# Fused attention and two feed-forward blocks: from step 21 the exponentials are transposed by VectorE and a trip through DRAM, not by TensorE

## The chip, the core and the metric

The program runs on one core of one Trainium2 chip. Its metric is device time in microseconds (us); the kernel before took 723.5 us (median of three runs, 723.3 to 726.39). The engines are named as in the profile: PE is TensorE's matmul pipe and PEld its weight loads, DVE is VectorE, ACT is ScalarE, POOL is GpSimd, and SP is the engine whose queue issues nearly all DMAs. Each engine works through its own instructions in a fixed order, and so does the queue of SP: an instruction that waits holds up all behind it.

## The reference, cut to what matters

```python
# q_l, k_l, v_l: 4 batches x 8 heads x 512 x 64;  q_g, k_g, v_g: 32 global tokens each
out_g = softmax(q_g @ [k_g, k_l].T / 8) @ [v_g, v_l]
s_ll  = where(|i - j| <= 32, q_l @ k_l.T / 8, -1e9)
out_l = softmax([q_l @ k_g.T / 8, s_ll]) @ [v_g, v_l]
x = concat(out_g, out_l)                 # 4 x 576 x 512
x = x + relu(layernorm(x) * g_ln @ w_ch1) @ w_ch2          # 512 -> 2048 -> 512
h = relu(x @ w_in)                                         # 512 -> 1024
c = conv over 3 neighbouring tokens of h, by channel (conv_w)
out = (h * sigmoid(c)) @ w_out                             # 1024 -> 512, all float32
```

A local query sees only 32 neighbours on each side and the 32 global keys. A tile of 128 queries thus needs 192 keys (an inner tile: 32 + 128 + 32) or 160 keys (an edge tile, the first and the last of a batch), and 32 global ones.

## The kernel before

The work is three overlapping parts. First, attention. It goes in *steps*: a `Local` step is a tile of 128 queries and one pair of heads, 64 of them (n = 0 to 63: batch, tile, pair), and a `Global` step is the 32 global queries of a batch and one pair, 16 of them, put between the local ones from n = 24 on. Steps 0 to 15 run alone at the start; the others run beside the second part. Second, the first network, in eight *chunks* of two or three tiles; each chunk goes through 16 blocks of weights (an *item* each: 12 matmuls into `ph`, ReLU by ACT into `hh`, the remainder into `hl` by DVE, then matmuls into `yps` one item later). Third, the second network.

A local step has these stages. The keys and queries are split into a high and a low part (`split`). PE writes the scores of both heads into `ps` (`products`), DVE adds the mask and finds the row's extreme (`sm`, `nm`), ACT makes the exponentials in place (`exps`). The values' product needs them with the keys on the partitions, so PE transposes `sm` against the identity, in three pieces of 128 keys for an edge tile and in four of 112 for an inner one (`turn`), ACT copies the result from PSUM to `ptsb` (`turned`), and PE multiplies it with `rawv` into `po` (`values`). After the fourth pair DVE divides by the sums and writes the tile `x` (`back`).

`add_step` says in which order the stages of neighbouring steps are written. In its step i it writes the scores of i, the transposes and the values of i-1 and the division of i-2, in four parts a to d. `tick` writes some of these parts after each piece of the first network, at a pace that gets a chunk's tiles ready by the chunk's start. All attention instructions get a priority that is 300 places ahead; a scheduler orders each engine's queue from priority, data and free buffers.

Tiles for the third chunk on are already transposed as the change does it: `cross` transposes the normalized tile in blocks of 32 x 32 on DVE into `stage`, a DMA writes it to DRAM (`way`), and four DMAs, one for each 32 partitions, read it back into `xn` with the blocks in their new places. There are 12 such trips. ACT and DVE then copy `xn` into `xe` or `xo`, the operand of `ph`.

Lines of the kernel before that the prediction speaks of: 321, 322 (scores), 325 (mask and extreme), 334 (exponentials), 347 (transposes by PE), 352 (their copy), 362 to 364 and 368 (values), 207, 210, 213 (the trip of `cross`), 109 (copies, of `xn` too), 760 (`ph`), 769 (`hh`), 770 (`hl`), 784, 785, 789 (`yps`), 164 (last use of the buffers `fpx` in converting weights). A matmul of float32 data such as the values' is two instructions in the trace; a transpose is one.

## Time and profile before

| | |
|---|---|
| three runs | 723.3, 723.5, 726.39 us |
| span of the profiled execution | 721.6 us (its own time is not listed apart; the median of the runs is 1.9 us longer than this span) |
| busy: PE, PEld | 709.5 us (98%), 637.1 us (88%) |
| busy: DVE, ACT, POOL | 455.8 us (63%), 424.0 us (59%), 173.2 us (24%) |
| mean granted TensorE clock | 0.999 of 2.4 GHz |
| chain that ended last | PE 87%, DMA 5%, DVE 2%, ACT 2% |
| DMA | 82.16 MB, mean busy share of the 16 engines 36% |

The profile is of one execution. A group of instructions has its count, its mean duration and the idle time of its engine just before it. A busy PE is not PE at its peak, since matmuls overlap: what one costs on a full PE is the distance from its start to the next start, and that is read from the timeline. In a row of the timeline the idle time stands at the end, with what ended it.

### The profile page before, as it was taken

Reading aid. Unit: us, or ns where it says so; the run is one execution under the profiler, and the core shown is the slowest. Engines: PE = TensorE matmul, PEld = TensorE weight load, DVE = VectorE, ACT = ScalarE, POOL = GpSimd, SP = SyncE. Lnnn points to the kernel's source line nnn. Section 1 sums busy time; section 2 is a strip of 40 time slices with the busy share of each in tenths; the row PEclk is TensorE's granted clock in tenths of the full one; section 3 lists DMA queues with packets and bytes.
Section 4 is the critical chain, followed back from the end, with each engine's and each line's share of the span. In section 5 each row is a group of like instructions: output and inputs, shape, how many; then the busy total and the mean of one; then the engine's idle time right before and its main releaser. Section 6 shows DMA issues by size and latency. Waiting matters only on the chain.

```text
span 721.6 us, 12952 instructions
## 1 busy us (share of the span) xinstructions
PE 709.5 (98%) x4617; PEld 637.1 (88%) x4617; DVE 455.8 (63%) x1132; ACT 424.0 (59%) x1003; POOL 173.2 (24%) x236
## 2 busy tenths in 40 slices
PE   9989999999999999999999999999999999999997
PEld 5778899989989999999899999899999888998985
DVE  3889971735554364555535543484888989889770
ACT  6859663566666666665556541252656776566561
POOL 1012021534344353543333410000001111201000
PEclk9999999999999999999999999999999999999999
DMA  9993231634453363336324310514601121110102
GB/s 369 424 419 94 72 125 54 151 116 115 116 140 102 102 148 118 114 99 159 118 71 93 118 57 1 145 59 106 277 25 39 63 74 15 63 59 1 59 1 73
DMA packets 72656, 82.16 MB, mean 114 GB/s; under 512 B 40064, under 2 KB 53136, under 8 KB 70032
## 3 DMA queue, kind: packets, MB, share of 16 engines
q1 hardware_dynamic: 72064, 80.64, 35.5%
q8 instruction: 36, 0.59, 0.4%
q10 hardware_dynamic: 528, 0.70, 0.3%
q14 instruction: 28, 0.23, 0.1%
HBM read 69.26 MB, written 12.06 MB: 113 GB/s over the span
## 4 chain that ended last, share of the span: by engine, by line
PE 87%; DMA 5%; DVE 2%; ACT 2%; issue 2%; SPq 1%; POOL 0%; DVEq 0%; ACTq 0%; POOLq 0%
PE ph L760 23%; PE yps L784 8%; PE yps L789 8%; PE yps L785 8%; PE po L1128 4%; PE po L1129 4%; PE po L1127 4%; PE pz L1056 3%; PE pv L1056 3%; PE px L1056 3%; PE po L368 3%; PE pt L347 3%; DMA wraw<-w 2%; PE py L1056 2%; PE pog L456 1%
## 5 line engine op out<-in xcount | busy, mean ns | idle before, releaser
L760 PE MATMUL ph<-xe,w 128*128 128x256 f32 (+1 forms) x768 | 118.8, 299 | 0.9 <-ACT w L160 0.9
L760 PEld LDWEIGHTS ph<-xe,w 128*128 128x128 f32 x768 | 107.7, 189 | 5.6 <-ACT w L160 1.2
L760 PE MATMUL ph<-xo,w 128*128 128x256 f32 x768 | 110.4, 284 | 0.0
L784 PE MATMUL yps<-w,hh 128*128 128x512 f32 x272 | 109.2, 401 | 1.2 <-ACT hh L769 0.7
L785 PE MATMUL yps<-w,hh 128*128 128x512 f32 x272 | 107.7, 396 | 0.0
L760 PEld LDWEIGHTS ph<-xo,w 128*128 128x128 f32 x768 | 101.7, 189 | 4.0
L116 POOL TENSOR_TENSOR kl<-raw,kh 128x448 fp32r<-128x448 f32 (+2 forms) x59 | 70.8, 1200 | 138.6 <-ACT kh L109 131.8
L769 ACT ACTIVATE hh<-ph 128x256 fp32r<-128x256 f32 (+1 forms) x128 | 50.1, 391 | 78.7 <-PE ph L760 73.1
L770 DVE SCALAR_TENSOR_TENSOR hl<-ph,hh 128x256 fp32r<-128x256 f32 x112 | 46.7, 417 | 62.8 <-ACT hh L769 62.2
L789 PE MATMUL yps<-w,hl 128*128 128x512 f32 x224 | 72.1, 397 | 0.0
L334 ACT ACTIVATE sm<-sm,nm 128x192 f32<-128x192 f32 (+1 forms) x128 | 58.5, 458 | 14.0 <-DVE nm L325 13.8
L784 PEld LDWEIGHTS yps<-w,hh 128*128 128x128 f32 x272 | 51.2, 188 | 8.7 <-ACT hh L769 1.5
L325 DVE CUSTOM_DVE_ANT_0 sm<-ps,mask 128x192 f32<-128x192 f32 (+1 forms) x128 | 42.5, 367 | 25.3 <-PE ps L322 13.9
L785 PEld LDWEIGHTS yps<-w,hh 128*128 128x128 f32 x272 | 51.3, 188 | 6.0
L1062 DVE SCALAR_TENSOR_TENSOR c<-hs,cw,c 128x544 f32<-128x544 f32 x64 | 48.9, 779 | 3.7 <-ACT c L1060 2.7
L1128 PE MATMUL po<-w,gh 128*128 128x512 f32 x128 | 50.8, 397 | 0.0
L1129 PE MATMUL po<-w,gl 128*128 128x512 f32 x128 | 50.7, 396 | 0.0
L1127 PE MATMUL po<-w,gh 128*128 128x512 f32 x128 | 50.6, 396 | 0.0
L109 ACT ACTIVATE kh<-raw 128x448 fp32r<-128x448 f32 (+2 forms) x59 | 34.2, 580 | 27.6 <-PE ps L321 16.2
L789 PEld LDWEIGHTS yps<-w,hl 128*128 128x128 f32 x224 | 41.1, 188 | 9.0 <-DVE hl L770 0.2
L352 ACT ACTIVATE ptsb<-pt 128x384 f32<-128x384 f32 (+1 forms) x64 | 34.4, 537 | 20.6 <-PE pt L347 20.0
L1069 POOL CAST grem<-gh 128x32 fp32r<-128x32 f32 x32 | 14.7, 458 | 120.6 <-ACT gh L109 120.6
(188 smaller groups left out, 1448.3 us busy)
## 6 DMA issues: line engine op xcount, KB each, us to landing
wraw<-w SPq DMA_DIRECT2D x16, 1024.0 KB, 16.9
raw<-a_m SPq DMA_DIRECT2D x23, 352.0 KB, 3.0
raw<-a_e SPq DMA_DIRECT2D x20, 320.0 KB, 2.9
raw<-g_qk SPq DMA_DIRECT2D x16, 304.0 KB, 2.8
rawg<-g_v SPq DMA_DIRECT2D x16, 280.0 KB, 2.9
wraw<-w_in SPq DMA_DIRECT2D x8, 512.0 KB, 4.8
wraw<-w_out SPq DMA_DIRECT2D x4, 1024.0 KB, 10.6
yscr<-x SPq DMA_DIRECT2D x60, 64.0 KB, 2.1
```

The lines of the kernel that those rows point to most:

```text
L116: return e_lo.tensor_tensor(lo, src, f32(hi), op=ALU.subtract)
L334: ACT.activation(s, s, AF.Exp, bias=self.nm[:, j:j + 1], scale=-1.0, accum_out=xt.sums[:, h:h + 1])
L760: e = PE.matmul(ph[:, :n], w[:, d * P:(d + 1) * P], x[:, d], start=m == 0, stop=m == 3 * NDC - 1)
L769: ACT.activation(hh, ph[:, :n], AF.Relu)
L784: PE.matmul(yps[i], hh[:, tk], wh[:, DM:], start=edge(k, -1), stop=False)
L785: PE.matmul(yps[i], hh[:, tk], wl[:, DM:], start=False, stop=False)
L789: mark["last"] = PE.matmul(yps[i], hl[:, tk], wh[:, DM:], start=False, stop=edge(k, 1)).ins
L1056: PE.matmul(ps, wx_, y[:, d], start=start and d + m == 0, stop=d + m == 3, skip_group_check=True)
L1062: named[k, b, f] = DVE.scalar_tensor_tensor(c, h[:, k:S + k], cw[:, 3 * f + k:3 * f + k + 1], c, op0=ALU.mult, op1=ALU.add)
L1127: PE.matmul(o, gh, wh, start=first, stop=False)
L1128: PE.matmul(o, gh, wl, start=False, stop=False)
L1129: PE.matmul(o, gl, wh, start=False, stop=last)
```

## The change

Local steps from n = 21 on (`far`; 23 inner and 20 edge ones) no longer use PE for the transposition. `leave`, after the exponentials, is one DVE transposition of 32 x 32 blocks from `sm` into one staging buffer and one DMA to DRAM. `arrive`, a step later, is four DMAs that read it back, one for each 32 partitions, into one of three buffers. `arrived`, one more step later, is an ACT copy that puts the 32-wide pieces in order, from SBUF to `ptsb`, in place of the copy from PSUM. The values are multiplied three steps behind their scores where it was one, and the division comes four behind where it was two. An inner tile's head now has 256 columns in `sm` of which 224 are filled, so its four products go over 128 and 96 keys where they went over 112 each; their number stays, and `rawv` is laid out and loaded to match. The staging buffer and the three landing buffers are the two `fpx` tiles, which hold weights being converted before and after. The step's `rawv` is loaded at `arrive`.

```diff
+FAR = 21
+LAG = 3
...
+            a, b = (mpool.tile([P, 2 * DM], F32, tag=f"fpx{k}", name="trip") for k in range(2))
+            trips.append([a[:, :DM]])
+            trips.append([a[:, DM:], b[:, :DM], b[:, DM:]])
...
+        def leave(self):
+
+            n = self.nc * P
+            stage = next_of(trip_homes()[0])[:, :n]
+            DVE.transpose(stage.rearrange("p (g m r) -> p m g r", g=NDC, r=SG),
+                          self.sm[:, :n].rearrange("p (m g r) -> p m g r", g=NDC, r=SG))
+            self.way = dram.tile([P, n], F32, tag=f"trip{self.nc}", name="trip", bufs=3)
+            SP.dma_start(self.way, stage)
+
+        def arrive(self):
+            n = self.nc * SG
+            pt = self.back_home = next_of(trip_homes()[1])[:, :self.nc * P].rearrange("p (k e) -> p k e", e=n)
+            y = self.way.rearrange("(k r) f -> r k f", r=SG)
+            for g in range(NDC):
+                SP.dma_start(pt[g * SG:(g + 1) * SG], y[:, :, g * n:(g + 1) * n])
+
+        def arrived(self):
+            self.pt = apool.tile([P, 5, P], F32, tag="pt", name="ptsb", bufs=PTB)[:, :self.nc]
+            ACT.activation(self.pt.rearrange("p m (k r) -> p m k r", r=SG),
+                           self.back_home.rearrange("p k (m r) -> p m k r", r=SG), AF.Copy)
...
-                    PE.matmul(po[:, j], self.pt[:c, k], v[:, k * D:(k + 1) * D], start=k % 2 == 0, stop=k % 2 == 1)
+                    c = (P, self.w - P)[k % 2] if self.far else self.c
+                    PE.matmul(po[:, j], self.pt[:c, k], self.rawv[:c, k * D:(k + 1) * D], start=k % 2 == 0, stop=k % 2 == 1)
...
+        def lag(k):
+
+            steps = at(i - k - LAG + 1), at(i - k)
+            return [s for s, far in zip(steps, (True, False)) if s and s.far == far]
...
         def a():
-            if one and not late:
-                one.transposes()
+            if near and not late:
+                near.transposes()
...
-            if two:
-                two.back()
+            for s in lag(2):
+                s.back()
...
         def b():
...
+            if one and one.far:
+                one.arrive()
+                one.loadv()
...
         def c():
-            if one and not late:
-                one.values()
+            for s in lag(1):
+                if not late or s.far:
+                    s.values()
             if cur:
                 cur.scores2()
+                if cur.far:
+                    cur.leave()
...
         def d():
...
+            for s in lag(0):
+                if s.far:
+                    s.arrived()
```

The scheduler gives the following queues. Line numbers of the changed kernel differ: 339 and 340 are the scores, 408 the values, 816 is `ph`, 825 `hh`, 840, 841 and 845 `yps`, 466 and 467 the scores of a global step, 497 its values.

PE before, from the values of a global step (`pog`) on; `pt` is the transposition of step 42, whose scores stand 24 rows higher, and `ps` here are a global step's scores:

```order
L789 MATMUL yps_3223<-w_713,hl_3484 128x512
L456 MATMUL pog_3466<-v_3406,ptsb_3427 128x256 x5
L347 MATMUL pt_3492<-ident_63,sm_99 112x128 x4
L425 MATMUL ps_3565<-kh_3519,xe_95 128x272
L426 MATMUL ps_3565<-kl_3520,xe_95 128x272
L760 MATMUL ph_3572<-xo_933,w_787 128x256 x8
```

PE of the change, after the scores of step 42; `po` are the values of step 41 (`ptsb_3467`) and of step 42 (`ptsb_3602`):

```order
L497 MATMUL pog_3452<-v_3389,ptsb_3399 128x256 x5
L816 MATMUL ph_3469<-xo_933,w_647 128x256 x8
L816 MATMUL ph_3469<-xo_934,w_647 128x256 x3
L408 MATMUL po_3447<-rawv_3344,ptsb_3467 128x64 x4
L816 MATMUL ph_3469<-xo_934,w_647 128x256
L816 MATMUL ph_3530<-xo_933,w_680 128x256 x8
L816 MATMUL ph_3530<-xo_934,w_680 128x256 x4
L408 MATMUL po_3447<-rawv_3513,ptsb_3602 128x64
L466 MATMUL ps_3583<-kh_3503,xe_95 128x272
L467 MATMUL ps_3583<-kl_3504,xe_95 128x272
L408 MATMUL po_3447<-rawv_3513,ptsb_3602 128x64 x3
```

The row with `pt` is gone from PE, and what stands between a step's scores and its values is now more of the first network.

SP before, about the same place: loads of a step's keys (`raw`) and values (`rawv`), stores of a tile (`yscr`), and one trip of `cross` (`way`, `xn`):

```order
L741 DMA yscr_70<-x_1437 32x16x32 x3
L396 DMA raw_3351<-g_qk 128x608
L741 DMA yscr_70<-x_1888 32x16x32
L282 DMA rawv_3290<-a_m 112x256
L741 DMA yscr_70<-x_1888 32x16x32 x3
L277 DMA raw_3435<-a_e 128x640
L210 DMA way_3241<-stage_1460 128x512
L277 DMA raw_3499<-a_e 128x640
L213 DMA xn_3233<-way_3241 32x4x128 x4
```

SP of the change at the same trip of `cross`, with the trips of steps 42 (`trip_3464`) and 43 (`trip_3528`) around it; `trip_1138` and `trip_1139` are the buffers in SBUF:

```order
L295 DMA raw_3622<-a_e 128x640
L374 DMA trip_3464<-trip_1138 128x512
L300 DMA rawv_3573<-a_m 128x256
L381 DMA trip_1138<-trip_3464 32x4x128 x2
L212 DMA way_3354<-stage_1572 128x512
L381 DMA trip_1138<-trip_3464 32x4x128 x2
L374 DMA trip_3528<-trip_1138 128x512
L215 DMA xn_3346<-way_3354 32x4x128 x4
L381 DMA trip_1139<-trip_3528 32x4x128 x4
```

Five DMAs for each far step have come in, and a read-back stands behind whatever was put before it.

ACT of the change there, with the ordering copies of steps 41 and 42 (line 385):

```order
L352 ACTIVATE sm_97,sums_3167<-sm_97,nm_3478 128x224
L385 ACTIVATE ptsb_3467<-trip_1139 128x512
L352 ACTIVATE sm_97,sums_3167<-sm_97,nm_3478 128x224
L385 ACTIVATE ptsb_3602<-trip_1138 128x512
L825 ACTIVATE hh_3499<-ph_3469 128x256
L825 ACTIVATE hh_3545<-ph_3530 128x256
```

In the place of a copy that waited for PE there is one that waits for four DMAs, and `hh` of the first network is queued behind it.

## Rows read from the trace of the kernel before

**Rows 1.** The page's part 1: busy us, share of the span, instructions.

```profile
PE 709.5 (98%) x4617; PEld 637.1 (88%) x4617; DVE 455.8 (63%) x1132; ACT 424.0 (59%) x1003; POOL 173.2 (24%) x236
```

**Rows 2.** Windows, 80 to 440 us, the stretch with the far steps.

```profile
core 0: us, PE busy (x) PEld busy (x) DVE busy (x) ACT busy (x) POOL busy (x), PEclk, DMA share, GB/s
80.00:440.00 360.00, 357.30 (x2474) 330.12 (x2472) 184.84 (x602) 217.00 (x588) 135.36 (x142) 1.00 0.39 107
```

**Rows 3.** Waits of PE, 80 to 440 us: in total, times, longest.

```profile
PE ps L321 <- DVE nm L429: 1.5, 1, 1.5
PE yps L784 <- ACT hh L769: 0.7, 1, 0.7
PE pog L456 <- DVE ptsb L451: 0.4, 1, 0.4
```

**Rows 4.** Timeline of PE, two places: start us, us, what.

```profile
287.60 0.60 PE L347 MATMUL pt<-ident,sm 128*112 128x128 f32 x4
287.95 0.37 PE L425 MATMUL ps<-kh,xe 128*128 128x272 f32 x1
288.17 0.29 PE L426 MATMUL ps<-kl,xe 128*128 128x272 f32 x1
288.29 1.58 PE L760 MATMUL ph<-xo,w 128*128 128x256 f32 x12
289.71 0.39 PE L784 MATMUL yps<-w,hh 128*128 128x512 f32 x1
...
322.03 0.49 PE L347 MATMUL pt<-ident,sm 128*128 128x128 f32 x3
322.35 0.39 PE L362 MATMUL po<-rawv,ptsb 128*128 128x128 f32 x2
```

**Rows 5.** Groups by form, 80 to 440 us: busy us, mean ns, idle before.

```profile
L347 PE MATMUL pt<-ident,sm 128*112 128x128 f32 x96 | 15.5, 272 | 0.0
L352 ACT ACTIVATE ptsb<-pt 112x512 f32<-112x512 f32 x24 | 14.3, 594 | 14.4 <-PE pt L347 14.1
L207 DVE STREAM_TRANSPOSE stage<-xn 128x128 f32<-128x128 f32 x44 | 9.7, 277 | 0.0
L737 DVE STREAM_TRANSPOSE x<-x 128x512 f32<-128x512 f32 x10 | 6.6, 684 | 0.0
L109 ACT ACTIVATE xe<-xn 128x512 fp32r<-128x512 f32 x6 | 3.8, 632 | 10.4 <-DMA xn<-way 10.4
L109 ACT ACTIVATE xo<-xn 128x512 fp32r<-128x512 f32 x4 | 2.5, 631 | 6.0 <-DMA xn<-way 6.0
```

**Rows 6.** Timeline of one trip of `cross`.

```profile
332.84 0.87 DVE L207 STREAM_TRANSPOSE stage<-xn 128x128 f32<-128x128 f32 x4
333.74 0.34 SPq L210 DMA_DIRECT2D way<-stage  x1
335.85 1.74 SPq L213 DMA_DIRECT2D xn<-way  x4
339.33 0.63 ACT L109 ACTIVATE xo<-xn 128x512 fp32r<-128x512 f32 x1 [2.06 <-DMA xn<-way]
```

**Rows 7.** Line 213, the read-backs of all trips: ns min, median, max.

```profile
L213 SPq DMA_DIRECT2D xn<-way x48: 302/424/1542, 142.3 to 461.3; - x48
DMA to landing us min/median/max: 1.8/2.1/3.6
```

**Rows 8.** Timeline of ACT: the longest wait for a trip.

```profile
416.21 0.63 ACT L109 ACTIVATE xe<-xn 128x512 fp32r<-128x512 f32 x1 [4.47 <-DMA xn<-way]
```

**Rows 9.** Timeline of step 43: its last score and its last exponential.

```profile
284.08 0.28 PE L322 MATMUL ps<-kl,xe 128*128 128x224 f32 x1
...
285.68 0.18 ACT L334 ACTIVATION_READ_ACCUMULATOR sm<-sm,nm 128x1 f32 x1
```

**Rows 10.** The tile `fpx`: its last use in converting weights.

```profile
L164 DVE TENSOR_TENSOR w<-fpx,w x8: 1209/1218/1223, 48.1 to 106.0; 128x1024 fp32r<-128x1024 f32 x8
```

**Rows 11.** Timeline of DVE: the division of the last tile.

```profile
454.28 0.69 DVE L378 TENSOR_TENSOR x<-po,rec 128x512 f32<-128x512 f32 x1 [1.17 <-DMA yscr<-x]
```

More of the change, by code (lines that the diff above doesn't have):

```diff
@@ L229, in stats, with trip_homes, next_of @@
             DVE.bn_aggr(self.mv, st)
+    trips = []
+    def trip_homes():
+        if not trips:
+            a, b = (mpool.tile([P, 2 * DM], F32, tag=f"fpx{k}", name="trip") for k in range(2))
+            trips.append([a[:, :DM]])
+            trips.append([a[:, DM:], b[:, :DM], b[:, DM:]])
+        return trips
+    def next_of(ring):
+        ring.append(ring.pop(0))
+        return ring[-1]
     home = apool.tile([P, 4 * P], F32R, tag="q2", name="qs")
@@ L252, in __init__ @@
             self.whole = n < WHOLE
+            self.far = n >= FAR
             self.key = b, t
@@ L257, in __init__ @@
             self.c, self.nc = (P, 3) if self.edge else (self.w // 2, 4)
+            self.pitch = 2 * P if self.far and not self.edge else self.w
             self.m0 = {0: SG + WIN, NT - 1: 0}.get(t, SG)
@@ L277, in load @@
             SP.dma_start(self.raw[:, :v], src[:, :v])
-            self.vsrc = src[:self.c, v:n]
+            self.vsrc = src[:, v:n]
         def loadv(self):
@@ L323, in products @@
             for j in range(2):
-                s = self.sm[:, j * w:(j + 1) * w]
+                s = self.sm[:, j * self.pitch:j * self.pitch + w]
                 DVE.tensor_tensor_reduce(out=s, in0=ps[j][:, :w], in1=mask[:, self.m0:self.m0 + w], scale=-0.125,
@@ L387, in tile_kernel @@
         key = "g"
+        far = False
         def __init__(self, b, hp):
@@ L538, in at @@
             return queue[k] if first <= k < len(queue) else None
-        cur, one, two = (at(i - k) for k in range(3))
-        three = queue[i - 3] if first - 1 <= i - 3 < len(queue) else None
-        ended = [t.key if t and ends(t) else None for t in (two, three, at(i - 4))]
-        norms = [k for k, far in zip(ended, (True, False)) if k and (place[k][0] > 1) == far]
-        turns, late_turns = ([k for k in ended[n:n + 1] if k and (place[k][0] > 1) == far] for n, far in ((1, False), (2, True)))
+        def lag(k):
+            steps = at(i - k - LAG + 1), at(i - k)
+            return [s for s, far in zip(steps, (True, False)) if s and s.far == far]
+        cur, one = at(i), at(i - 1)
+        near = one if one and not one.far else None
+        three = queue[first - 1:first] if i - 3 == first - 1 else lag(3)
+        ended = [[t.key for t in ts if ends(t)] for ts in (lag(2), three, lag(4))]
+        norms = [k for ks, far in zip(ended, (True, False)) for k in ks if (place[k][0] > 1) == far]
+        turns, late_turns = ([k for k in ended[n] if (place[k][0] > 1) == far] for n, far in ((1, False), (2, True)))
         after, third, fourth = (at(i + k) for k in (1, 2, 3))
@@ L548, in a @@
         def a():
-            if one and not late:
-                one.transposes()
+            if near and not late:
+                near.transposes()
             if fourth:
                 fourth.load()
-            if third and i > first:
+            if third and i > first and not third.far:
                 third.loadv()
@@ L563, in b @@
             if late:
-                one.transposes()
+                near.transposes()
+            if one and one.far:
+                one.arrive()
+                one.loadv()
             for key in late_turns:
@@ L570, in c @@
         def c():
-            if one and not late:
-                one.values()
+            for s in lag(1):
+                if not late or s.far:
+                    s.values()
             if cur:
                 cur.scores2()
+                if cur.far:
+                    cur.leave()
         def d():
             if late:
-                one.values()
+                near.values()
+            for s in lag(0):
+                if s.far:
+                    s.arrived()
             if cur:
@@ L592, in tile_kernel @@
     micro.append(order[first].split)
-    for i in range(first, len(queue) + 4):
+    for i in range(first, len(queue) + 3 + LAG):
         add_step(i)
@@ L697, in tile_kernel @@
     for s in sms:
-        POOL.memset(s[D:, LOCAL:], 0.0)
+        POOL.memset(s[:, LOCAL:], 0.0)
     def products(i):
@@ L1204, in _layout, with window @@
     Z = np.float32
-    def window(t):
+    def window(t, far=False):
         lo, hi = max(0, t * P - WIN), min(SL, (t + 1) * P + WIN)
@@ L1226, in window @@
             pad[:, :, :, 3] = vv[:, :, 2 * P:]
+        elif far:
+            v2 = vv.reshape(B, NP, 2, w, D).transpose(0, 1, 3, 2, 4)
+            pad[:, :, :, 0::2] = v2[:, :, :P]
+            pad[:, :, :w - P, 1::2] = v2[:, :, P:]
         else:
@@ L1232, in _layout @@
     a_e = np.stack([wins[0], wins[3]], 1)[1:]
-    a_m = np.stack([wins[1], wins[2]], 1)[1:]
+    a_m = np.stack([window(1, True), window(2, True)], 1)[1:]
     a_w = np.zeros((2, NT, NP, P, RWH), Z)
```

2 lines of the change are left out of this document (1 added, 1 removed).

## The prediction, made before the changed kernel ran

> **What bounds the kernel now.** I read the page first: PE is busy 98% of the span, the other three engines 24 to 63% [rows 1]. A high share alone does not say that removing work from PE shortens the run, so the next view is the stretch with the far steps, 80 to 440 us. There PE is busy 357.3 of 360 us, DVE 184.8 and ACT 217.0, and the granted clock is 1.00, the upper level of 2.4 GHz [rows 2]. The third view, PE's waits in that stretch, has three entries of 2.6 us in total [rows 3]. So in 360 us PE almost never waits for anything: whatever else is slow there is hidden, and the length of the stretch is the sum of PE's own distances from start to start.
>
> **What a transposition costs on a full PE.** By duration it is 272 ns [rows 5], but durations overlap. The timeline has the distance: four transpositions start at 287.60, the matmul after them (425) at 287.95 and the one after that (426) at 288.17 [rows 4]. Line 425 took 0.22 us to its successor where 426, of the same size, took 0.12, so 0.10 of the first is still the transpositions' cost. Four of them cost 288.17 - 287.60 - 0.12 = 0.45 us, or about 0.44 with the first network's own pace, 1.42 us for 12 matmuls [rows 4], as the yardstick. Three of an edge tile take 322.35 - 322.03 = 0.32 us, with float32 matmuls behind them [rows 4].
>
> In its section "Reading a trace" (Performance Expectations) the Trainium skill's page Trainium Kernel Development and Optimization says that busy time of matmuls is a bad measure, because they are pipelined. The trace agrees: 272 ns by duration against 0.11 by distance. By the durations, 152 x 0.272, the change would take off 41 us, by the distances 16.5; the sum goes by the distances.
>
> **The change part by part.**
>
> *Transpositions off PE.* 23 inner steps x 0.44 = 10.1 us and 20 edge steps x 0.32 = 6.4 us: 16.5 us less on PE, all of it in the stretch where PE has no slack. The rest of PE's queue is the same set of instructions: an inner step's four products go over 128 and 96 keys in place of 112 and 112, and the number of columns, which sets their pace, stays.
>
> *DVE.* 43 more transpositions. One of 512 columns took 684 ns, four of 128 columns 0.87 us [rows 5, 6]; edge tiles have 384. That is between 43 x 0.55 = 24 and 43 x 0.87 = 37 us (0.55 is an estimate, 684 scaled down to 384 columns with a little left over); I take 28. DVE goes from 184.8 to about 213 of some 343 us. It is hidden by PE as long as `hl` (line 770) is in time. New on DVE is that it waits for ACT's exponentials and, with one staging buffer, for the landing of the previous write; `hl` and the masks of later scores queue behind. That wait has no row; below I price it with the trip.
>
> *ACT.* A copy of 512 columns from PSUM took 594 ns, the ordering copy of `xn` from SBUF, the same kind of access, 632 [rows 5]: 43 x 0.04 = under 2 us, hidden (217 of 360 busy). What counts is that this copy now waits for four DMAs, with `hh` (line 769) queued behind it.
>
> *The trip against its room.* The trip of `cross` shows all its parts [rows 6]: DVE ends at 333.71, the write is issued at 333.74, the first read-back at 335.85, four take 1.74 us of the queue, and ACT starts at 339.33: 5.6 us. From the last score's end to the last exponential it took 285.86 - 284.36 = 1.5 us in step 43 [rows 9]. With 0.7 for the scores, 0.7 for DVE, 0.6 for the copy and about half a microsecond for the handovers, a far step needs some 9.6 us from its first score to its first value when nothing queues. I measured its room by walking the changed kernel's PE queue with the distances of rows 4: 11 of the 43 steps have 10.9 to 12.5 us, 9 have 12.5 to 15.5, and 23 have more. So no step is short by the plain chain, 11 are tight if a queue adds 1.5 us or more, and step 42, shown in the order, is one of these (11.1 us, with the write of `cross` between its read-backs).
>
> How late do such trips come, and what does it do to PE? In this stretch ACT waited 16.4 us for the read-backs of ten trips [rows 5], up to 4.47 us for one, with nothing on PE at that time [rows 3, 8]: `hh` has slack because `yps` of an item comes after `ph` of the next. Had all 2.6 us of PE's waits been due to those ten trips, it would be 0.26 us for each. The bounds are thus 0 (all trips covered, and with them perhaps the 1 us of waits that went through the old copies and banks recovered) and 43 x 0.26 = 11 us. I take the 11 tight steps at 0.26, 3 us: nearer to the lower end because the other 32 have more room than the trips of `cross` needed.
>
> *SP's queue.* A trip occupies SP from 333.74 to 335.85 + 1.74, 3.85 us, of which some 1.8 are waiting for the write, where another load may stand in between, as in the order. Over 43 trips that is 166 of 360 us on top of the loads before. In the last ten steps, 54 to 63, the changed queue has 84 issues; at a median of 0.42 [rows 7] they take 35 us, and with the ten write waits bare 53, while PE's queue gives 45 us from the first of their values to the last. Mean load is bearable, the last steps are at the edge; inside the 0 to 11 us above I count nothing apart for it.
>
> *The late division and the `fpx` buffers.* Tiles come two steps later in the order of writing, and the pace brings the attention forward for it: in the order at step 42 it stands beside the weights of three items earlier. The last tile's division waited for a store of `x` at the chunk's change, not for its values [rows 11], so a slightly later end of the attention costs nothing. The trips of steps 22 and 23 need `fpx`, which the weights leave after 106 [rows 10]; the order gives the three first far steps 14.9 to 25 us of room. Cost 0, and up to 3 us if the trip of step 22 queues behind the weights.
>
> **The sum.** The profiled span is 721.6 us, 1.9 below the median of the runs, and I keep this distance. 723.5 - 16.5 + 3 = 710.
>
> **The rivals.**
>
> *A. The trips are late more widely.* All 43 cost what the ten of before could at most have cost, 11 us: 723.5 - 16.5 + 11 = 718. For it: one staging buffer ties DVE to SP's queue, and SP's is longer. Against it: the 23 steps with over 15.5 us of room.
>
> *B. SP's queue becomes the bound, and the run slower.* It decides from the point where the work that SP has for a far step, 3.85 us of trip plus its loads and stores, exceeds the distance of far steps: 360 / 43 = 8.4 us on average, 4.5 in the last ten. Then each trip comes later than the one before, the values of a step stand in PE's queue without data, and PE waits at each of them. An excess of 0.5 us a step is 43 x 0.5 = 21.5 us: 723.5 - 16.5 + 21.5 = 728.5. For it: the last ten steps (35 to 53 us against 45), read-backs that land after 3.6 us at the longest [rows 7], and loads that stand behind a waiting read-back. Against it: over the whole stretch there is room, since the steps there are twice as far apart as at the end.
>
> The Trainium skill's page VectorE: DVE Perf Modes (Rules for kernel authors) is on this side: a 128 x 128 transposition belongs on TensorE if its result may go to PSUM, and the vector engine does only 32 x 32 blocks. Here the blocks are put in order by DMA at 5.6 us a trip in place of 0.44 us on PE, so that by the rule the change only loses; the trace agrees that the trip is far longer, and not that PE is the cheaper place, since PE is the one engine with no slack.
>
> *C. PE gains nothing because ACT takes its place.* ACT's waits for trips, at 1.64 us each as in the ten of before, are 43 x 1.64 = 71 us; with 217 busy that is 288 of 343 us. If `hh` then sets the pace, the gain is eaten and the time is 723. For it: an ACT that is 84% taken has bursts in which it is late. Against it: the wait of 4.47 us that nobody felt.
>
> **How the numbers follow.** A measurement of this kernel can tell a change from none from about 0.5%, 3.6 us. Forecast (706 to 714): 0.62. A, or a part of it (714 to 720): 0.18, and that is still faster. C, or A with the last ten steps late too: 0.11, within 3.6 us. B: 0.09. Faster 0.80, the same 0.11, slower 0.09. The range: below, 723.5 - 16.5 - 1 for the recovered waits, 706; above, it takes in A and the beginning of C, 721. By itself the forecast has 706 to 714.
>
> **What would show it right or wrong.** Right: PE transposes `sm` for the steps up to 20 only, PE's instructions fall by 152, PE is still busy over 97% from 80 to about 425 us, and its waits there are a few us, at the values of line 408 or at `yps`. ACT has waits for `trip` of 1 to 2 us each, DVE has 43 transpositions from `sm` at 0.55 to 0.87 us. Wrong: PE waits for `ptsb` at line 408 step after step (A, and B if SP's queue shows each trip issued later after its DVE end than the one before, above all in steps 54 to 63), or at `yps` for `hh` with ACT held by `trip` (C). Also wrong if the second half, after the attention, is longer than before by more than a few tenths: I expect it unchanged but earlier.

## The result: slower, 733.7 us, and the profile after

The changed kernel takes 733.67 us (median of four runs, 732.19 to 738.13), the kernel before 723.79 on the same chip. The ratio is 1.0146 with a 95% interval of 1.0122 to 1.0169: 10 us slower where 13.5 us faster was forecast, and outside the range. The profiled span is 731.2 us against 721.6. Two executions among the runs below took some 2% longer than their kernel's others, at a lower mean granted clock (e11_bare's profiled one, 727.1 us, and one of the kernel before, 741.3), and are left out of medians and ratios.

The first lines are from the page after, its part 1 (as [rows 1]) and the chain of work that ended last, by engine; then the window of the far steps (as [rows 2]) and the worst 40 us in it.

```profile
PE 703.5 (96%) x4465; PEld 623.4 (85%) x4465; DVE 478.5 (65%) x1175; ACT 422.5 (58%) x1003; POOL 173.6 (24%) x236
...
PE 55%; DMA 22%; DVE 7%; ACT 5%; SPq 5%; issue 4%; POOL 0%; ACTq 0%; DVEq 0%; POOLq 0%
```

```profile
80.00:440.00 360.00, 341.91 (x2262) 308.32 (x2261) 206.28 (x642) 213.95 (x584) 135.77 (x142) 0.99 0.57 161
280.00:320.00 40.00, 35.19 (x222) 31.55 (x221) 21.15 (x72) 23.44 (x65) 15.61 (x17) 0.92 0.54 163
```

PE has its 152 instructions less (4617 to 4465). But in 80 to 440 us it is idle for 18.1 us instead of 2.7. The six largest waits of PE in that stretch (in total, times, longest), where [rows 3] had three entries of 2.6 us:

```profile
PE yps L840 <- ACT hh L825: 4.9, 5, 2.3
PE po L408 <- ACT ptsb L385: 4.7, 5, 1.9
PE po L401 <- ACT ptsb L385: 3.2, 3, 1.3
PE yps L845 <- DVE hl L826: 1.4, 2, 1.2
PE ps L339 <- DVE nm L343: 1.4, 3, 0.8
PE ps L466 <- DVE nm L343: 1.1, 2, 0.6
```

Only 7.9 us are the values themselves (lines 408 and 401). As much again stands elsewhere: at `yps` for ACT's `hh` and DVE's `hl`, and at scores whose bank DVE hasn't emptied. What PE waits for there is an engine that stands in order at something else. The page's groups and SP's longest wait show at what:

```profile
L385 ACT ACTIVATE ptsb<-trip 128x512 f32<-128x512 f32 (+1 forms) x43 | 24.9, 578 | 44.5 <-DMA trip<-trip 40.4
L371 DVE STREAM_TRANSPOSE trip<-sm 128x512 f32<-128x512 f32 (+1 forms) x43 | 27.8, 646 | 32.4 <-ACT sm L352 17.2
```

```profile
SPq L381 <- DMA trip<-trip: 46.6, 33, 2.9
```

The 43 ordering copies held ACT idle for 44.5 us, 40.4 of them at read-backs, besides their 24.9 us of work; the 43 transpositions held DVE for 32.4 us, 17.2 of them at exponentials that weren't finished and, by DVE's waits, 13.4 at the one staging buffer.

To count what PE lost, waits alone don't do, since a slower pace is no wait. I took every distance from one start to the next on PE, less the median distance of the same kind of instruction in the kernel before, and summed over 80 to 460 us: 5.1 us in the kernel before, 29.4 in the one after. I call this PE's lost distance below. 23 of the 29 us lie in 120 to 320 us. From the start of the last matmul of `ph` (line 760 before, 816 after) to the end both kernels take the same, 187.9 and 187.8 us.

PE's longest stand, 2.33 us, is not at a far step's trip. ACT stood 3.11 us at a trip of `cross`, which the kernel before has too, and `hh` came late behind it:

```profile
314.44 0.63 ACT L111 ACTIVATE xe<-xn 128x512 fp32r<-128x512 f32 x1 [3.11 <-DMA xn<-way]
...
316.98 0.79 PE L840 MATMUL yps<-w,hh 128*128 128x512 f32 x1 [2.33 <-ACT hh L825]
```

In the kernel before ACT waited 4.47 us for such a trip at 416 us [rows 8], and PE's only wait for `hh` in the stretch, 0.7 us [rows 3], stands at 344 us.

### One step in full: step 42

The timeline of the kernel after, with the rows of DVE, SP, ACT and PE that belong to step 42, whose last score ended at 273.83:

```profile
277.10 0.69 DVE L418 TENSOR_TENSOR x<-po,rec 128x512 f32<-128x512 f32 x1 [2.46 <-DMA yscr<-x]
278.43 0.69 DVE L371 STREAM_TRANSPOSE trip<-sm 128x512 f32<-128x512 f32 x1
...
279.15 0.34 SPq L374 DMA_DIRECT2D trip<-trip  x1
282.62 0.80 SPq L381 DMA_DIRECT2D trip<-trip  x2
283.51 0.38 SPq L212 DMA_DIRECT2D way<-stage  x1
283.95 0.91 SPq L381 DMA_DIRECT2D trip<-trip  x2
...
287.19 0.63 ACT L385 ACTIVATE ptsb<-trip 128x512 f32<-128x512 f32 x1 [0.89 <-DMA trip<-trip]
287.84 0.66 ACT L825 ACTIVATE hh<-ph 128x256 fp32r<-128x256 f32 x2
...
284.24 1.78 PE L816 MATMUL ph<-xo,w 128*128 128x256 f32 x13
287.87 0.43 PE L408 MATMUL po<-rawv,ptsb 128*128 128x64 f32 x2 [1.86 <-ACT ptsb L385]
```

The exponentials were done at 275.7. The transposition started 2.7 us later, because DVE stood at a division that waited for a store of `x`; the first read-back came 3.5 us after the write instead of the 2.1 us of [rows 6]; the write of `cross` went between the read-backs, as the order had shown; the copy began 8.1 us after DVE's end instead of 5.6, and two `hh` evictions were behind it. From the first score's start (273.23) to the first value 14.6 us passed, and the order gave 11.1.

Read in the same way for all 43 steps, the trip from DVE's end to the last landing has a median of 7.6 us (5.5 to 11.5). The write is issued 0.9 us after DVE's end in the median (0.03 in [rows 6]), and the first read-back 2.65 us after the write (2.11 there). Up to ACT's start the median is 9.05 us, but for 19 of the 43 copies ACT had hardly a wait, under 0.1 us: the data had mostly landed before the copy's turn came. From the first score's start to the last exponential it took 3.15 us in the median.

What followed is in the windows of 2 us (busy time of PE, PEld, DVE, ACT, POOL, then PE's granted clock, DMA share, GB/s):

```profile
286.00:288.00 2.00, 0.14 (x2) 0.13 (x2) 0.44 (x2) 1.08 (x3) 0.00 (x0) 1.00 0.54 186
288.00:290.00 2.00, 2.00 (x13) 1.86 (x14) 1.20 (x4) 1.73 (x5) 0.81 (x1) 0.84 0.49 139
290.00:292.00 2.00, 2.00 (x7) 1.61 (x7) 0.81 (x3) 1.43 (x4) 1.07 (x2) 0.50 0.25 69
292.00:294.00 2.00, 2.00 (x14) 1.91 (x14) 0.30 (x2) 0.30 (x2) 0.00 (x0) 0.81 0.92 278
```

PE stood, then ran with a granted clock of 0.50, the lower level of 1.2 GHz, before it got back to 1.00. Matmuls of the same form show it by their starts, 0.42 us apart at the lower level and 0.23 after it:

```profile
289.78 0.63 PE L840 MATMUL yps<-w,hh 128*128 128x512 f32 x1
290.20 0.63 PE L841 MATMUL yps<-w,hh 128*128 128x512 f32 x1
...
293.47 0.39 PE L840 MATMUL yps<-w,hh 128*128 128x512 f32 x1
293.70 0.39 PE L841 MATMUL yps<-w,hh 128*128 128x512 f32 x1
```

A stand of 1.9 us so cost another 1.7 (the sum of 2 us times what the clock lacks to 1). Over 80 to 460 us the kernel after lost 3.4 us in this way at two places, the kernel before none.

### The profile page after: what moved, and what is told of

Same layout as the page of the kernel before. It is cut to its first block, busy times and chain, and to the rows that moved or that the text cites. A ratio compares the mean times of both kernels' runs of the same rounds, so it can differ in the third digit from the quotient of the medians.

```text
span 731.2 us, 13045 instructions
## 1 busy us (share of the span) xinstructions
PE 703.5 (96%) x4465; PEld 623.4 (85%) x4465; DVE 478.5 (65%) x1175; ACT 422.5 (58%) x1003; POOL 173.6 (24%) x236
## 4 chain that ended last, share of the span: by engine, by line
PE 55%; DMA 22%; DVE 7%; ACT 5%; SPq 5%; issue 4%; POOL 0%; ACTq 0%; DVEq 0%; POOLq 0%
PE ph L816 13%; DMA trip<-trip 7%; DMA wraw<-w 5%; PE yps L840 5%; PE yps L845 4%; PE yps L841 4%; PE po L1184 4%; PE po L1185 4%; PE po L1183 4%; DMA way<-stage 4%; PE pz L1112 3%; PE pv L1112 3%; PE px L1112 3%; DMA xn<-way 2%; SPq L215 2%
## 5 line engine op out<-in xcount | busy, mean ns | idle before, releaser
L816 PE MATMUL ph<-xe,w 128*128 128x256 f32 (+1 forms) x768 | 116.6, 297 | 0.9 <-ACT w L162 0.9
L816 PE MATMUL ph<-xo,w 128*128 128x256 f32 x768 | 104.9, 283 | 0.0
L816 PEld LDWEIGHTS ph<-xo,w 128*128 128x128 f32 x768 | 99.9, 190 | 3.9
L352 ACT ACTIVATE sm<-sm,nm 128x192 f32<-128x192 f32 (+1 forms) x128 | 58.4, 458 | 12.1 <-DVE nm L343 11.9
L385 ACT ACTIVATE ptsb<-trip 128x512 f32<-128x512 f32 (+1 forms) x43 | 24.9, 578 | 44.5 <-DMA trip<-trip 40.4
L371 DVE STREAM_TRANSPOSE trip<-sm 128x512 f32<-128x512 f32 (+1 forms) x43 | 27.8, 646 | 32.4 <-ACT sm L352 17.2
```

What stands on the lines that cost most here:

```text
L352: ACT.activation(s, s, AF.Exp, bias=self.nm[:, j:j + 1], scale=-1.0, accum_out=xt.sums[:, h:h + 1])
L816: e = PE.matmul(ph[:, :n], w[:, d * P:(d + 1) * P], x[:, d], start=m == 0, stop=m == 3 * NDC - 1)
```

## The experiments

Theory A: TensorE's gain is real, and values and copies that come to their place in the order before the trip is through eat it. Rivals: B, the trips cost by transfers and SP's queue wherever the values stand; D, TensorE wasn't the pace, and any work taken off it turns into waits; L, values that come later cost by themselves; S, VectorE standing in order is the cost. (In the expectations A' is A's first half, TensorE as the pace, and R its second, the room; C and S' are forms of S, with the staging buffer and with ScalarE's copy; T puts the loss in the even steps.) All medians are beside runs of the kernel before on the same chip (723.8 to 724.1 us). PE's lost distance is of the one profiled run.

| run | us | ratio to before, 95% interval | PE's lost distance, us |
|---|---|---|---|
| e12_one_of_four | 708.6 | 0.978 (0.976 to 0.980) | 2.9 |
| e11_bare | 711.5 | 0.983 (0.982 to 0.985) | not taken |
| e11b_bare3 | 712.6 | 0.984 (0.982 to 0.986) | 11.0 |
| e28_own_ring | 720.2 | 0.994 (0.992 to 0.996) | 18.6 |
| e23_idle_turns | 722.2 | 0.998 (0.997 to 0.999) | 4.5 |
| e18_lag_only | 724.3 | 1.000 (0.999 to 1.001) | 5.0 |
| e17_no_trip_late | 724.4 | 1.001 (0.999 to 1.003) | 23.8 |
| e1_no_trip | 726.8 | 1.003 (1.002 to 1.005) | 23.7 |
| e15_lag4_leave_late | 728.1 | 1.006 (1.004 to 1.008) | 25.3 |
| e21_lag4_late_pool | 728.3 | 1.007 (1.004 to 1.009) | 24.6 |
| e27_odd_only | 728.8 | 1.006 (1.004 to 1.008) | 15.7 |
| e13_idle_trips | 729.2 | 1.006 (1.005 to 1.008) | 11.5 |
| e14_lag4_stage2 | 733.1 | 1.013 (1.011 to 1.014) | 28.0 |
| e3_behind | 734.3 | 1.011 (1.008 to 1.015) | 32.9 |
| e8_lag4 | 735.8 | 1.016 (1.014 to 1.018) | 32.0 |
| e2_stage2 | 738.1 | 1.019 (1.018 to 1.021) | 34.0 |
| e10_dead | 743.2 | 1.026 (1.024 to 1.029) | 25.8 |
| e9_lag2 | 743.9 | 1.028 (1.026 to 1.029) | 41.6 |

### Is the gain on TensorE real?

**e12_one_of_four**, an edit of the kernel before:

```diff
-            for k in range(self.nc):
+            for k in range(self.nc if self.n < 21 else 1):
                 PE.transpose(self.pst[:c, k], self.sm[:, k * c:(k + 1) * c], ident)
...
-            ACT.activation(self.pt[:c], self.pst[:c, :self.nc], AF.Copy)
+            got = self.pst[:c, :self.nc] if self.n < 21 else self.pst[:c, :1].to_broadcast([c, self.nc, P])
+            ACT.activation(self.pt[:c], got, AF.Copy)
```

> The kernel before, with one transposition a step on TensorE instead of three or four from step 21 on (109 fewer); the eviction keeps its length by reading the one square repeatedly, so every other engine's work and all waits keep their kind. It leaves out that the other squares are transposed. No trips, no late values. Theory A' (TensorE paces 120 to 440 us, so work taken off it shows in full): 109 x 0.109 = 12 us less, 711 to 713 us. Theory D (the other engines' chains pace these 300 us nearly as tightly; work taken off TensorE turns into waits): 719 to 724 us.

708.6 us, 15.3 less; by the profiled spans 721.6 - 707.9 = 13.7. The forecast's distance gives 109 x 0.109 = 11.9, and the waits of PE, which also shrank, the rest. The window of the far steps, and all of PE's waits in it:

```profile
80.00:440.00 360.00, 359.39 (x2457) 331.19 (x2457) 188.49 (x611) 218.32 (x593) 135.78 (x142) 1.00 0.40 109
```

```profile
PE po L363 <- ACT ptsb L353: 0.4, 1, 0.4
PE ps L426 <- DVE nm L325: 0.2, 1, 0.2
```

Theory D falls: TensorE is the pace, and with early values the other engines can follow at 708.6 us.

**e10_dead**, the kernel after with the transpositions back as dead work:

```diff
                 near.transposes()
+            if one and one.far:
+                one.turn()
```

> The kernel after with the removed transpositions put back on TensorE as dead work (three or four a step into a bank that nothing reads). Theory A' (losses by the trips stand beside what TensorE does): 733.7 + 16.5 = 748 to 751 us. Theory D (TensorE only waits where it has got ahead; the dead work fills its waits): 733 to 739 us.

743.2 us: between the two. Of the 16.5 us, 9.5 show by the medians (5 to 12 by the two intervals; 13.8 by the profiled spans, 745.0 - 731.2, but that run of e10_dead is the longest of six). So a part of the dead work fell into stands of PE, and most of the stands stayed: the lost distance is 25.8 us against 29.4.

### What do the parts cost without each other?

**e18_lag_only**: TensorE transposes at once, the squares wait in four buffers, only the values come late.

```diff
+            if one and one.far:
+                one.transposes()
...
-                    cur.leave()
...
+                    with tc.issue_after(scored[-1]) if s.far else nullcontext():
+                        s.values()
```

> TensorE's transpositions and ScalarE's eviction as in the kernel before, at their early place; only the values come three steps behind their scores and not ahead of the latest scores (the evicted squares stand in four buffers of their own until then). No VectorE transposition, no trip. Theory L (lateness itself costs: a tile's division, normalization and hidden layer come two steps later, and what is planned right behind them waits): 728 to 735 us. Theory that lateness is free: 722 to 725 us.

724.3 us, no change; theory L falls.

**e23_idle_turns** and **e13_idle_trips**, the kernel before with VectorE's transposition added, without and with the DMAs (SP's write in `leave`, the four read-backs in `arrive`):

```diff
             if cur:
                 cur.scores2()
+            if isinstance(cur, Local) and cur.n >= 21:
+                cur.leave()
...
+            if isinstance(one, Local) and one.n >= 21:
+                one.arrive()          # e13 alone
```

> The kernel before with the 43 transpositions of the exponentials on VectorE added, into four buffers in turn that nothing reads; no write and no read-back, so e13_idle_trips without its transfers. If VectorE's 28 us in order cost: 727 to 730 us. If the staging buffer's wait for its write and the transfers cost: 723 to 725 us.

> The kernel before with 43 trips added that nobody waits for: VectorE's transposition into the staging buffer, the write and the four read-backs, at the places where the kernel after has them; TensorE's transpositions, their eviction and the early values stay. Theory B (the trips cost by VectorE's 28 us, their transfers and their rows in SP's queue): 728 to 735 us. Theories A' and D: the trips themselves cost next to nothing, 723 to 726 us.

722.2 us: VectorE's 28 us are hidden, even a little better than nothing. 729.2 with the transfers: 5.3 us more than before, and 7.0 more than e23_idle_turns, though nobody waits for the data. Waits of DVE in e13_idle_trips, 80 to 440 us:

```profile
DVE trip L369 <- DMA trip<-trip: 23.8, 16, 4.4
DVE trip L369 <- ACT sm L350: 11.6, 14, 1.2
```

DVE stands 23.8 us until the write before has left the one staging buffer, and PE waits among others 1.6 us at `yps` for `hl`. In e23_idle_turns DVE stood as long at exponentials (23.5 us, 30 times, longest 1.2) and PE lost nothing: many short stands were absorbed there, and those of e13_idle_trips are longer (4.4 us at most). How the 5.3 us divide between that buffer and the transfers' share of SP and the DMA engines is open.

From here the loss can be added up: 723.9, + 5.3 for the trips alone, + 14.0 for copies and values that depend on them (e10_dead less e13_idle_trips, both with a full TensorE), - 9.5 for the transpositions gone = 733.7. The terms are sure to 1 to 4 us by their intervals, and hold for this order of adding: with the 16.5 us taken off whole first, as in the forecast, the trips cost 733.7 - 723.5 + 16.5 = 26.7.

### Is it the room between scores and values?

**e9_lag2** and **e8_lag4** change the steps between scores and values (in e8 the values' operands are loaded a step later):

```diff
-LAG = 3
+LAG = 2      # e9
+LAG = 4      # e8
```

> Values are written two steps behind their scores instead of three; nothing else is changed. In TensorE's order nearly every room is then 9.5 to 14 us where half of them were 15 to 20. Theory A: a chain of 12 to 14 us doesn't fit in 30 or more steps; 30 steps by about 1 us more: 745 to 770 us. Theory B or C: 731 to 737 us, as after.

> Values are written four steps behind their scores instead of three (the values' operands are loaded a step later, so that three buffers do). The trips, their number, bytes and queue stay. In TensorE's order the narrowest rooms between scores and values grow from 11 to 12 us in 11 steps to 16 to 20 us in nearly all. Theory A (room too small for a trip): 708 to 716 us, ScalarE's waits for arrived trips fall from 44 us to under 15. Theory B (the trips cost by their transfers and their rows in SP's queue, wherever the values stand): 730 to 736 us as after. Theory C (ScalarE's and VectorE's own chain with one staging buffer): 728 to 735 us.

With less room 743.9, as theory A says in kind (745 to 770): ACT's copies wait 63.9 us instead of 38.5. With more room A expected 708 to 716, and it became 735.8. A row each of ACT, DVE and PE in e8_lag4:

```profile
ACT ptsb L385 <- DMA trip<-trip: 16.1, 6, 3.7
...
DVE trip L371 <- DMA trip<-trip: 19.9, 12, 2.8
...
PE ps L339 <- DVE nm L470: 6.0, 3, 3.7
```

The copies' wait did fall, from 38.5 to 16.1, and PE's waits for `ptsb` from 7.9 to 1.2. In their place PE waits for scores banks that DVE empties late, and DVE stands at the staging buffer. So A falls as the whole cause: when one stand went, others took its place.

**e3_behind** keeps three steps, but forbids TensorE and ScalarE to run ahead:

```diff
+                    with after_step(scored, getattr(s, "n", -9) + 2) if s.far else nullcontext():
+                        s.values()
...
+                    with after_step(expd, s.n + 2):
+                        s.arrived()
```

> Values three steps behind as in the kernel after, but TensorE may not take them ahead of the scores of two steps later, nor ScalarE the ordering copy ahead of those exponentials. The narrowest rooms grow from 11 to 12 us to 13 to 14.5, the others stay. Theory A: the 11 tight steps lose some 2 us less each, 716 to 726 us. Theory B: 731 to 736 us.

734.3 us, as after, where A expected 716 to 726. The copies' waits fell here too, from 38.5 to 21.3 us, and PE's at `yps` for `hh` rose from 4.9 to 7.9.

### Is it VectorE standing in order?

**e2_stage2**, **e14_lag4_stage2** (that and LAG = 4) and **e15_lag4_leave_late** (that, with the transposition behind the masks of the next step; the read-backs also go one step later, which the cut leaves out):

```diff
-            trips.append([a[:, :DM]])
-            trips.append([a[:, DM:], b[:, :DM], b[:, DM:]])
+            trips.append([a[:, :DM], b[:, :DM]])
+            trips.append([a[:, DM:], b[:, DM:]])
...
-                if cur.far:
-                    cur.leave()
+            if one and one.far:                    # e15
+                with tc.issue_after(masked[-1]):
+                    one.leave()
```

> The kernel after with two staging buffers and two landing buffers instead of one and three; nothing else is changed. VectorE then needn't wait until the write of the step before has left the buffer (13.4 us in 12 waits in the kernel after). Theory S (VectorE standing at the staging buffer, with the second halves of the hidden layer and the masks behind it in order, is a large part of the loss): 726 to 730 us. Theory R (values and copies reach their places before a trip is through, whatever VectorE does): 732 to 735 us.

> Values four steps behind (as e8_lag4) and two staging buffers. Theory S: with the room wide, VectorE's 20 us at the staging buffer were what kept e8_lag4 at 735.8; without them 720 to 727 us. Theory that wide rooms cost by themselves (later divisions, normalizations and hidden layers): 731 to 736 us.

> As e14_lag4_stage2, and the transposition on VectorE is moved one step of the queue later, behind the masks of that step, so that VectorE doesn't stand at exponentials that ScalarE hasn't finished (14 to 16 us in e8_lag4 and after); write and read-backs move with it. Theory S (what stands in VectorE's order is the loss): another 3 to 6 us below e14_lag4_stage2, 716 to 722 us. Theory R: the trips end later, the copies wait again, no better or worse than e14_lag4_stage2 by up to 8 us.

e2_stage2 took VectorE's wait at the staging buffer away and gained nothing: 738.1, 4 us more than the kernel after. DVE now stood 24.2 us at exponentials instead of 17.2, and the copies still waited 33.1 us. It also has one landing buffer less, so it isn't clean. In e14_lag4_stage2 a copy reads its landing buffer only after the read-back of two steps later has gone into it, so its copies wait for a later trip; its 733.1 us tell nothing of theory S. In e15_lag4_leave_late that isn't so, since the read-backs moved too: 728.1, 7.7 us under e8_lag4. DVE's transposition now waits 7.6 us in total, and the staging buffer has no row. But SP's waits for a trip's write, beside those of e8_lag4, fell with it:

```profile
SPq L381 <- DMA trip<-trip: 48.1, 36, 3.3
...
SPq L384 <- DMA trip<-trip: 29.1, 26, 3.0
```

So S may hold for a part; how much of the 7.7 us is VectorE's and how much SP's, these runs don't tell. e15 is the fastest full version of the new path, and slower than the kernel before.

**e21_lag4_late_pool** takes e15's copy off ScalarE:

```diff
-            ACT.activation(self.pt.rearrange("p m (k r) -> p m k r", r=SG),
-                           self.back_home.rearrange("p k (m r) -> p m k r", r=SG), AF.Copy)
+            POOL.tensor_copy(self.pt.rearrange("p m (k r) -> p m k r", r=SG),
+                             self.back_home.rearrange("p k (m r) -> p m k r", r=SG))
```

> As e15_lag4_leave_late (728.1 us), and the ordering copy is GpSimd's instead of ScalarE's. If ScalarE's standing at trips that aren't through (16 us there) with hidden-layer evictions behind it is a part of the loss: 719 to 725 us. If not, or if GpSimd's longer copies and what stands behind them (second halves of keys and values) cost as much: 727 to 735 us.

728.3 us: no gain. GpSimd's copies were as long as ScalarE's (609 ns against 614 in the median), and PE's waits for `hh` fell from 3.9 to 1.6 us. But GpSimd now stood 18.7 us at trips and 12.0 for a shared `ptsb` buffer, with second halves of keys and values behind it; whether that cost what ScalarE's stands had cost, the run doesn't tell.

### What is left without the DMAs?

**e1_no_trip** (no write, no read-back; the copy reads the staging buffer), **e17_no_trip_late** (that, with the values behind the latest scores) and **e28_own_ring** (that, with buffers of their own for the copies):

```diff
-            SP.dma_start(self.way, stage)
+            self.back_home = stage.rearrange("p (k e) -> p k e", e=self.nc * SG)
...
-            self.pt = apool.tile([P, 5, P], F32, tag="pt", name="ptsb", bufs=PTB)[:, :self.nc]
+            self.pt = next_of(trip_homes()[1])[:, :self.nc * P].rearrange("p (k e) -> p k e", e=P)   # e28
```

> The kernel after without its 43 trips: the write to DRAM and the four read-backs of a step are left out, the ordering copy reads the staging buffer itself (so the exponentials that are multiplied have their squares transposed but not moved). VectorE's transposition, ScalarE's copy and TensorE's order of work stay. Theory A (the work taken off TensorE is worth what was forecast, and all of the loss is TensorE and ScalarE standing in order behind data still on the trip): 723.5 - 16.5 + 2 = 706 to 711 us, next to no wait of the ordering copy. Theory B (the order itself, VectorE's longer chain or the removed transpositions being hidden already keeps it slow): 720 to 733 us.

> e1_no_trip (no write, no read-backs; VectorE's transposition and ScalarE's copy stay; four staging buffers) with the values not ahead of the latest scores, three steps behind, as in e11b_bare3: rooms of 13 to 16 us instead of 6 to 12. Leaves out the trip through DRAM. Theory R (narrow rooms cost, not the work): 711 to 716 us, as e11b_bare3. Theory S' (VectorE's 28 us and ScalarE's copy standing in order behind the exponentials cost wherever the values are): 721 to 727 us, as e1_no_trip.

> As e17_no_trip_late (VectorE's transposition, no write and no read-back, ScalarE's copy, values not ahead of the latest scores; the trip through DRAM is left out), but the copies go to two buffers of their own instead of the two that they share with the global exponentials; two staging buffers remain. If ScalarE standing with a copy for a shared buffer (6 us there) and what follows is the loss: 712 to 717 us. If not: 722 to 726 us.

Without any DMA 726.8 us, 7 under the kernel after, and PE still loses 23.7 us, 6.8 of them by the granted clock. This surprised me most. The 7 us are not the price of the transfers alone: here 10 of the 43 values stand only 6 to 10 us behind their first scores, since the order is made anew for the shorter chain; putting nearly all back to 13 us or more (e17) gives 724.4. ACT then stands 6.1 us (5 times) with a copy for one of the two `ptsb` buffers that local and global steps share, and buffers of their own give 720.2 (this edit has two staging buffers instead of four as well).

**e11b_bare3** and **e11_bare** leave nothing between exponentials and values, three and two steps late:

```diff
+                if s.far:
+                    s.pt = s.sm[:, :s.nc * P].rearrange("p (k e) -> p k e", e=P)
...
-                    cur.leave()
-                one.arrive()
-                    s.arrived()
```

> The kernel after with nothing between exponentials and values from step 21: no transposition on any engine, no trip, no ordering copy; the values read the exponentials' own tile, three steps behind and not ahead of the latest scores (rooms 13 to 16 us). It leaves out the transposition itself; two more tiles for exponentials, each cleared once, let them stand longer. Theory A' (TensorE paces; its waits in the kernel after come from trip, staging and copy alone): 705 to 710 us. Theory D: 717 to 724 us, with waits on TensorE for other releasers (hidden layer, scores, global scores).

> As e11b_bare3 (nothing between exponentials and values: no transposition, no trip, no copy; the transposition is left out) with the values two steps behind instead of three. Theory L: between the 712.6 us of three steps and the some 703 us that e12_one_of_four points to without any lateness (708.6 less its last 43 transpositions): 705 to 710 us. Theory that lateness is free: 711 to 714 us, or above, since narrower rooms can only wait more.

712.6 and 711.5: lateness of two or three steps is the same here too. But with all 152 transpositions gone it should be some 707; PE loses 11.0 us, the largest at global scores for DVE (1.7 and 1.5). Late values were free with TensorE full (e18_lag_only). That they are not quite free when it is 16 us ahead would fit the 5 us, but isn't shown: no run has this kernel with early values.

### Is it the even steps?

**e27_odd_only**:

```diff
-            self.far = n >= FAR
+            self.far = n >= FAR and n % 2 == 1
```

> The kernel after with the new path in the odd steps alone (22 of 43); the even steps, the first of each pair, go the old way: transposed on TensorE at once, evicted, multiplied one step later. The odd steps' rooms are 12 to 20 us, their trips follow each other by 11 us or more, so one staging buffer is always free. Theory T (the loss sits in the even steps' narrow rooms and in trips that come in pairs): some 78 transpositions x 0.14 = 11 us are kept, 2 to 4 us lost: 713 to 718 us. Theory that each trip costs alike: half of after's +10: 727 to 730 us.

728.8 us. In this kernel a tile's last step comes after the next tile's first values, which go to the same bank, so products of two tiles are mixed and the order in that bank isn't that of a usable version. With this limit: the copies waited only 6.7 us (3 times), the clock never fell, and half the steps still cost half of what all cost (4.7 of 9.9 us). So the loss doesn't sit in the even steps' narrow rooms alone.

## Why the prediction was wrong, point by point

**Transpositions off PE, 16.5 us:** right as to PE. 152 instructions are gone, and e12_one_of_four shows the gain at or above the forecast's distance where nothing else is moved. In the changed kernel some 9.5 us of it show (e10_dead).

**DVE, 28 us, hidden:** 43 transpositions took 27.8 us, and alone they cost nothing (e23_idle_turns). The clause that DVE waits "for the landing of the previous write", with `hl` and masks behind, was named and then not priced by itself. e13_idle_trips and e15_lag4_leave_late point to several us in it, but neither has it alone, and e2_stage2, which only took that wait away, gained nothing.

**The trip against its room: the step that failed.** It took one trip of `cross`, 5.6 us in a quiet place, for all 43; to the last landing that one took 5.5, among the shortest of the twelve of the kernel before (5.4 to 7.8, median 6.3), and the 43 have a median of 7.6. It took 2.2 us from first score to last exponential from step 43 alone; the median is 3.15. With the rest of its chain the 9.6 us become some 12.5, longer than the room of the 11 tight steps (10.9 to 12.5). And it priced each tight step at 0.26 us, 3 us in all, with 43 x 0.26 = 11 us as the upper bound. The measured size is 19.3 us (5.3 + 14.0), or 26.7 in the place of that 3 in its own sum, above the bound either way. The 0.26 came from ten trips whose waits ACT could absorb, one at a time; with the far steps' waits beside them even a trip of `cross` cost PE 2.33 us (316.98). And the room on PE was compared with the plain chain alone, where the queues in between add their own stands, as step 42 shows for DVE's at 277.10 and SP's at 283.51. How the 14.0 us divide among the queues stays open.

**SP's queue and rival B (728.5 us):** its sign was right and its price nearest, its place wrong. It needed trips that come later and later, above all in steps 54 to 63; there the writes of steps 60 and 61 were issued 2.9 and 5.0 us after DVE's end, and their trips took 11.8 and 10.5 us up to ACT's start, but step 62 was back at 0.5 and 5.8: a queue built up and emptied again. The loss sits mostly in 120 to 320 us. SP stood 46.6 us at writes, and without any transfer the kernel is still at 726.8 us.

**Rival C (ACT takes over):** ACT's waits for trips are 40.4 us instead of the 71 feared, and e21_lag4_late_pool, without them on ACT, shows no gain. `yps` did wait for `hh`, 4.9 us in all, 2.3 of them behind a trip of `cross`. **Rival A (718):** the late trips were there, at more than its price.

**The rule on the vector engine's transposition** (the Trainium skill, VectorE: DVE Perf Modes, Rules for kernel authors), that a 128 x 128 transposition belongs on TensorE if its result may go to PSUM, gave the right sign: 733.7 us against 723.8. PE's work was not free here, since one of four transpositions there gave 708.6 us; what lost was the trip that puts the blocks in order, with its waits.

**The second half:** unchanged, as forecast, but 9.7 us later instead of earlier.

**Left open.** Why the chain without DMAs stays 8 to 14 us above the bare one (e28_own_ring, e17_no_trip_late and e1_no_trip against e11b_bare3); the shared `ptsb` buffers may be about 4 of it. No experiment took the trips off SP's queue, where their issue already comes late, so SP's part is not told apart from that of the values' places. None tried the order that the scheduler would make if it took the trips to be 8 us long.

## What to carry to other kernels

Where one engine is 98% full, the others work in the time that its length gives them. A gain on it and a longer chain beside it must be priced together, not one after the other: alone the gain showed whole (e12_one_of_four), beside the trips 9.5 of 16.5 us did. Count an added dependency at every queue that it passes in order (here DVE, SP, ACT and PE), with a trip's time taken from where the queues are loaded, and don't scale up from a few waits that nobody felt. Parts that cost nothing alone (late values 724.3, idle transpositions 722.2) say little of the whole; the run that adds them without their use (e13_idle_trips, e10_dead) shows where the sum breaks.

## What the runs showed of the hardware

The granted clock fell to 0.50 after some of PE's stands: after those of 1.86 and 2.3 us in the kernel after, where 3.4 us were lost in all; e9_lag2, whose PE stood most, lost 8.5 us so, and the kernel before, e12_one_of_four and e18_lag_only nothing. The forecast held a wait to cost its own length; here the two longest cost nearly twice that.

43 trips, a write and four read-backs each, whose data nobody uses slowed the kernel by 5.3 us (e13_idle_trips, 729.2), while the same 28 us of VectorE's work without them were free (e23_idle_turns, 722.2). Whether the staging buffer, SP's queue or the transfers cost it is open.
